# Copying a block's attention sums from PSUM with ScalarE or with VectorE, in 21 steps of a two-attention kernel

## Chip, cores and metric

The kernel runs on one core of one Trainium2 chip. Its time is that of one execution on the device in microseconds (us), and the figure for a kernel is the median of several executions. The profile is of one more execution.

## Reference

Two attentions over separate inputs, each S = 2048 positions by D = 576, with 32 heads of 18 columns. Their outputs stand side by side, so the result is 2048 x 1152. All of it is float32.

```python
# A: each position sees itself and 7 earlier ones, two apart
off = jnp.arange(8) * 2
idx = pos[:, None] - off[None, :]
logits = einsum("bhsd,bhswd->bhsw", q, k[idx]) * Dh ** -0.5   # masked where idx < 0
a = einsum("bhsw,bhswd->bhsd", softmax(logits), v[idx]) @ wo
# B: full attention
scores = einsum("bhqd,bhkd->bhqk", q, k) * Dh ** -0.5
b = einsum("bhqk,bhkd->bhqd", softmax(scores), v) @ wo
return concatenate([a, b], axis=-1)
```

Both begin with qkv = x @ wqkv (576 x 1728). A is called the local attention below.

## The kernel before, in words

**First phase** (to about 450 us): all projections, with each operand split into two parts whose products are added up, so that float32 accuracy is kept on TensorE. Queries, keys and values go to DRAM and come back in the layout of the second phase. The first maxima of the second phase are already made beside the projections.

**Second phase**: 512 steps. The 32 heads are 8 groups `g` of four; the queries are 4 blocks `b` of 512; the keys are 16 tiles `kt` of 128. Step 16 (4 g + b) + kt handles one tile of keys for one block of queries and four heads:

- `score` (L370 to L403) makes four products of keys and queries, 128 x 512 each, into PSUM banks. ScalarE takes the exponentials of them: two scores go through one bank each ("single", L398), two through a double bank and one instruction ("pair", L401).
- `maximum` and `first_part` (L322 to L362, reductions at L256, L258 and L272) make scores of a later block once more, and VectorE reduces them to maxima over the keys, which that block's exponentials need. An ordinary step has three of these: two whole ones ("A" and "B", one on each half of TensorE's rows, r = 0 and 1) and one in two halves ("D" then "E", where E holds the reduction, L272).
- `weigh` (L867 to L874) multiplies the exponentials of the step before with the values: four products (L870) into four partition ranges of the PSUM tile `po`, summed over the 16 key tiles. There is one `po` only. A row of ones in the values makes the softmax denominator.

The order in an ordinary step is written out by hand in `PLAIN = "D1AzwE2B"` (L48; digits and letters w to z are scores), followed by the weigh of the step before. TensorE's rows are used in two halves, so that two matmuls run at once. The banks go round in fixed rings in such steps.

When the sixteenth weigh of a block is through, which is in step 16 (4 g + b + 1), `finish` (L876 to L912) is called in the same step. It copies `po` to the tile `o` (two buffers) in SBUF, and the next weigh, which starts `po` anew, has to wait for that copy. Then, by an agenda: SyncE loads the denominators out of `o` one step later (L904), VectorE inverts them 8 steps later, GpSimd multiplies `o` by them 18 steps later (L908), and the parts are stored to DRAM. The very last block goes another way (`closing`), so 31 blocks are copied.

**Output products of A.** GpSimd does most of the local attention; its results come back from DRAM as tiles `at` (L1090) and are multiplied with the output weights by `sums_of_a` (L1100 to L1119): two halves of the sum (L1211) in two banks, one for each half of the rows. ScalarE copies one half (L1110), VectorE adds the other (L1114). Such a product stands in a step of its own choice of order, from `ROWS` (L50), and `TURNS` (L56) lists the steps in which it may stand, among them every step 16 n: the step in which a block is also copied. `producing` collects the steps that have such a product, from the local attention (L1150) or, in the last group, from B's own output product. The exponentials of the local attention (L1041) take two steps of ScalarE's time, one if a product stands there.

In the steps with a product, `in_turn` (L1217) merges the two halves' queues of instructions: it keeps a clock for each half of TensorE's rows and for ScalarE and VectorE, in which `filled` and `emptied` (L157 to L168) book estimated durations, and always takes the half that could go first. `bank` (L95) then takes the bank that comes free first by these clocks. So a number booked for an engine can change the order and the banks in later steps of this kind.

Of the kernel before, what the change touches and what calls it, by code (L numbers as in the profile page):

```python
# [10 lines left out]
AF = mybir.ActivationFunctionType  # L11
# [40 lines left out]
GAP = 55  # L52

A_FROM = 10
# [4 lines left out]
def ap(t, *dims):  # L59

    return bass.AP(tensor=t.tensor, offset=t.offset, ap=[list(t.ap[0])] + [list(d) for d in dims])


def rows(t, *dims):

    return bass.AP(tensor=t.tensor, offset=t.offset, ap=[list(d) for d in dims])
# [3 lines left out]
def two_attentions(ctx: ExitStack, tc, xa, wa, woa, xb, wb, wob, out):  # L70
# [5 lines left out]
    nc = tc.nc  # L76
# [77 lines left out]
    def held_as(t):  # L154
        return next((n for n, h in held.items() if h is t), None)
# [6 lines left out]
    def emptied(engine, ns, r, t):  # L162

        busy[engine] = max(busy[engine], busy[r] + 214) + ns
        n = held_as(t)
        if n is not None:
            del held[n]
            freed[n] = busy[engine] + 100  # L168

    po = p_po.tile([128, 512], F32, name="po")  # L170
# [10 lines left out]
    step = 0  # L181

    def later(n, f):
        agenda[step + n].append(f)

    def plan(start, pieces):
        for n, f in pieces:
            agenda[start + n].append(f)
# [319 lines left out]
    with (tc.tile_pool(name="x", bufs=1, side="right") as xp,  # L508
# [346 lines left out]
        step = 0  # L855
# [11 lines left out]
    def weigh(*steps):  # L867
        for g, b, kt, es in steps:
            for i in range(4):
                nc.tensor.matmul(po[32 * i : 32 * i + 19], vs[g][:, kt, 19 * i : 19 * i + 19], es[i],  # L870
                                 start=kt == 0, stop=kt == NT - 1)
        busy[0] = busy[1] = max(busy[0], busy[1]) + 870 * len(steps) + 332
        if kt == NT - 1:
            finish(g, b)  # L874

    def finish(g, b):  # L876
        o = work.tile([128, 512], F32, name="o", bufs=2)
        if g == NG - 1 and b == NB - 1:
            return closing(b, o, work.tile([128, 512], F32, name="rec", bufs=1))
        nc.vector.tensor_copy(o, po)  # L880
        emptied("DVE", 598, 0, None)
        den = work.tile([128, 16], F32, name="den", bufs=2)
        rec = work.tile([128, 512], F32, name="rec", bufs=1)
        parts = []

        def room():
            if g == NG - 1 and b == 0:

                parts[:] = [ap(work.tile([128, 4, 128], F32R, name=f"at{i}", bufs=1), (1, 512)) for i in range(2)]
            else:  # L890
                n = work.tile([128, 2, 512], F32R, name="n", bufs=1)
                parts[:] = n[:, 0], n[:, 1], n
            return parts

        if g == NG - 1 and b > 0:
            return shortly(b, o, rec, *room()[:2])

        def store():
            if g < NG - 1:
                load(do[:, g, :, 512 * b : 512 * b + 512].rearrange("i p n -> p i n"), parts[2].bitcast(F32))  # L900
            else:
                plan(step, full(b, parts))

        for at, f in ((1, lambda: load(den, o[DH:128:32])),  # L904
                      (8, lambda: nc.vector.reciprocal(den, den)),
                      (9, lambda: load(drec[g, b].rearrange("i (p n) -> (i p) n", n=16), den)),
                      (13, lambda: load(rec, rows(drec[g, b], (512, 4), (0, 32), (1, 512)))),
                      (18, lambda: nc.gpsimd.tensor_mul(o, o, rec)),  # L908
                      (19, lambda: nc.gpsimd.tensor_copy(room()[0], o)),
                      (20, lambda: nc.gpsimd.tensor_sub(parts[1], o, parts[0])),  # L910
                      (26, store)):
            later(at, f)  # L912

    def shortly(b, o, rec, hi, lo):

        def halved(cols):
            nc.gpsimd.tensor_copy(hi[:, cols], o[:, cols])
            nc.gpsimd.tensor_sub(lo[:, cols], o[:, cols], hi[:, cols])


        cols = [slice(256 * i, 256 * i + 256) for i in range(2)]
        apart = b == 1
        for i in range(2):
            later(1 + i * apart, lambda i=i: nc.vector.transpose(rec[:, cols[i]], o[:, cols[i]]))
        later(1 + 2 * apart, lambda: divided(rec))
        for i in range(2):
            later(1 + (3 + i) * apart, lambda i=i: nc.vector.transpose(o[:, cols[i]], rec[:, cols[i]]))
            later(1 + (3 + i) * apart, lambda i=i: halved(cols[i]))
        plan(step, [(at + 2, f) for at, f in full(b, (hi, lo))])
# [15 lines left out]
    def closing(b, o, rec):  # L945

        n = work.tile([128, 2, 512], F32R, name="n", bufs=1)
        first(3, b, 1)
        for t in range(4):
            if t % 2 == 0:  # L950
                inverse(po, rec, slice(128 * t, 128 * t + 256), o)
            cols = slice(128 * t, 128 * t + 128)
            hi, lo = n[:, 0, cols], n[:, 1, cols]
            nc.scalar.activation(hi, o[:, cols], AF.Copy)
            nc.gpsimd.tensor_sub(lo, o[:, cols], hi)
        for t in range(4):
            end(t, b, (n[:, 0], n[:, 1]))
# [4 lines left out]
    producing = set()  # L962
# [325 lines left out]
    def full(b, new):  # L1288
        def half(t, h):
            if total - int(sum(given)) > 4:  # L1290
                inside.append(lambda: among(*quarter(t, h)))
            else:
                waiting.append(lambda: alone(*quarter(t, h)))

        def among(queues, end):
            behind_scores.append(end)
            return queues

        def quarter(t, h):
            if h == 0:  # L1300
                ys[t, b] = work.tile([128, D], F32, name="y", bufs=4)
            if h == 1:
                later(1, lambda: load(out[512 * b + 128 * t : 512 * b + 128 * t + 128, D:], ys[t, b]))
            return sum_of(ys[t, b][:, 288 * h : 288 * h + 288], t, h, [*olds[b], new])

        return [(4 + 2 * t + h, lambda t=t, h=h: half(t, h)) for t in range(4) for h in range(2)]
# [137 lines left out]
```

## Time and profile before

| | |
|---|---|
| median of 3 runs | 1590.14 us (1588.71 to 1592.66) |
| profiled execution, its own time | 1589.66 us |
| its span in the trace | 1587.8 us |
| TensorE busy | 1577.4 us |
| VectorE busy | 1399.7 us |
| ScalarE busy | 1180.6 us |
| GpSimd busy | 961.6 us |
| copies of `po` (L880), VectorE | 31, 21.3 us busy, 689 ns each |

PE in the rows is TensorE's matmul, PEld its weight load, DVE VectorE, ACT ScalarE, POOL GpSimd, SP SyncE; SPq is SyncE's instruction queue. A row of the timeline gives start and length in us, engine, line, operation, out<-in with the shapes, and how many instructions of the kind were merged into the row; in brackets the engine's idle time ahead of it and what ended that. Matmuls are pipelined, two at once on the two row halves, so the length of a merged PE row isn't the sum of its parts. In the chain of waits a row is what the last chain of work went through.

### The profile page before, as it was taken

What the parts mean: (1) busy time and instruction counts of PE and PEld (TensorE: products, weight loads), DVE (VectorE), ACT (ScalarE), POOL (GpSimd) and SP (SyncE); (2) the same over time, 40 slices, a digit from 0 to 9 for tenths busy, and PEclk for the clock granted to TensorE, in tenths of its full rate; (3) what the DMA queues carried; (4) which work ended last, traced back from release to release, by engine and by line L of the source; (5) the groups of instructions that cost most, each with busy time, mean ns of one, the idle gap of its engine ahead of it and who ended that gap; (6) DMA issues with size and microseconds to landing.
All of it is one profiled execution on the core that took longest, in us unless ns stands there. A gap on an engine that the chain in (4) does not pass through costs nothing.

```text
span 1587.8 us, 34762 instructions
## 1 busy us (share of the span) xinstructions
PE 1577.4 (99%) x13436; PEld 971.1 (61%) x13436; DVE 1399.7 (88%) x2381; ACT 1180.6 (74%) x1912; POOL 961.6 (61%) x816
## 2 busy tenths in 40 slices
PE   9999999999999999999999999999999999999998
PEld 7999999999544444444444445444445445455776
DVE  5299999999999999999998999999999999999433
ACT  6324441121699999999998999999999999998444
POOL 2305752201157997994994995995995997940100
PEclk9999999999999999999999999999999999999999
DMA  9848954532322253253236225324613232234211
GB/s 258 222 142 207 274 171 124 146 98 76 75 52 58 63 115 90 69 127 113 60 83 167 52 76 134 104 50 107 143 53 91 70 87 78 61 125 157 85 39 60
DMA packets 190149, 173.12 MB, mean 109 GB/s; under 512 B 123120, under 2 KB 136944, under 8 KB 188256
## 3 DMA queue, kind: packets, MB, share of 16 engines
q1 hardware_dynamic: 185120, 159.36, 36.1%
q0 software_dynamic: 4032, 10.63, 3.2%
q8 instruction: 105, 1.72, 0.5%
q10 hardware_dynamic: 832, 0.92, 0.2%
q14 instruction: 60, 0.49, 0.1%
HBM read 97.47 MB, written 72.95 MB: 107 GB/s over the span
## 4 chain that ended last, share of the span: by engine, by line
PE 97%; DVE 2%; DMA 1%; issue 0%; ACT 0%; POOL 0%; SPq 0%; ACTq 0%; DVEq 0%; POOLq 0%
PE po L870 31%; PE bank L239 20%; PE bank L491 17%; PE bank L388 10%; PE bank L1211 8%; PE pair L388 7%; PE bank L424 4%; DVE mx L256 1%; DMA at<-dao 0%; DVE mx L272 0%; DVE o L880 0%; PE bank L643 0%; DVE mx L258 0%; DMA out<-y 0%; PE bank L1189 0%
## 5 line engine op out<-in xcount | busy, mean ns | idle before, releaser
L239 PE MATMUL bank<-ks,qs 54*128 54x256 f32 (+1 forms) x2526 | 754.6, 372 | 1.0 <-ACT ohi L819 0.9
L256 DVE TENSOR_REDUCE mx<-bank 128x1 f32<-128x512 f32 x1024 | 680.1, 684 | 63.8 <-PE bank L239 39.6
L239 PEld LDWEIGHTS bank<-ks,qs 54*128 54x128 f32 x2526 | 414.2, 184 | 424.3 <-DVE mx L272 305.0
L398 ACT ACTIVATE e<-bank 128x512 f32<-128x512 f32 x1024 | 610.1, 602 | 71.5 <-PE bank L388 64.4
L870 PE MATMUL po<-ee,v 128*19 128x512 f32 x2048 | 537.1, 599 | 1.0 <-DVE o L880 0.2
L870 PE MATMUL po<-e,v 128*19 128x512 f32 x2048 | 531.8, 599 | 0.0
L401 ACT ACTIVATE ee<-pair 128x1024 f32<-128x1024 f32 x478 | 487.2, 1019 | 0.9 <-PE pair L388 0.3
L388 PE MATMUL bank<-qs,ks 56*128 56x512 f32 x1092 | 461.0, 442 | 0.0
L258 DVE TENSOR_REDUCE mx<-bank 128x2 f32<-128x512 f32 x546 | 356.5, 684 | 19.5 <-PE bank L239 6.6
L272 DVE TENSOR_REDUCE mx<-bank 128x2 f32<-128x512 f32 x478 | 326.1, 682 | 0.0
L388 PE MATMUL pair<-qs,ks 56*128 56x512 f32 x956 | 248.7, 396 | 0.0
L388 PEld LDWEIGHTS bank<-qs,ks 56*128 56x128 f32 x1092 | 194.6, 184 | 15.9 <-ACT e L398 9.0
L1062 POOL TENSOR_TENSOR pr<-lg,akv 128x1024 f32<-128x1024 f32 x72 | 157.0, 2200 | 0.6
L819 ACT ACTIVATE ohi<-bank 128x512 f32<-128x512 f32 (+1 forms) x56 | 30.4, 595 | 156.4 <-issue 129.1
L388 PEld LDWEIGHTS pair<-qs,ks 56*128 56x128 f32 x956 | 138.1, 185 | 0.1
L870 PEld LDWEIGHTS po<-ee,v 128*19 128x19 f32 x2048 | 69.6, 96 | 112.0 <-issue 108.1
L491 PE MATMUL bank<-xhi,ahi 64*128 64x512 f32 (+1 forms) x448 | 120.2, 390 | 0.0
L491 PE MATMUL bank<-xhi,alo 64*128 64x512 f32 (+1 forms) x448 | 114.5, 390 | 0.0
L491 PE MATMUL bank<-xlo,ahi 64*128 64x512 f32 (+1 forms) x448 | 108.8, 391 | 0.1
L1014 POOL TENSOR_TENSOR pr<-aq,akv 128x1024 f32<-128x1024 f32 x40 | 87.8, 2202 | 18.3 <-PE bank L239 17.1
L1064 POOL TENSOR_TENSOR pr<-pr 128x512 f32<-128x512 f32 x72 | 91.1, 1285 | 0.6
L539 POOL TENSOR_TENSOR alo<-raw,ahi 128x512 fp32r<-128x512 f32 (+1 forms) x14 | 17.6, 1257 | 117.4 <-ACT ahi L538 86.0
(206 smaller groups left out, 2383.7 us busy)
## 6 DMA issues: line engine op xcount, KB each, us to landing
do<-n SPq DMA_DIRECT2D x28, 512.0 KB
da<-ohi SPq DMA_DIRECT2D x52, 256.0 KB
akv<-da SPq DMA_DIRECT2D x64, 175.5 KB
out<-y SPq DMA_DIRECT2D x32, 288.0 KB
qs<-dqk SPq DMA_DIRECT2D x30, 288.0 KB
ks<-dqk SPq DMA_DIRECT2D x30, 288.0 KB
at<-dao SPq DMA_DIRECT2D x64, 128.0 KB
rec<-drec SPq DMA_DIRECT2D x29, 256.0 KB
```

The source lines that it names most:

```text
L239: return nc.tensor.matmul(ps, qs[rows_, b, p, 128 * t : 128 * t + 128], ks[rows_, p, 512 * k + at : 512 * k + at + n], start=True, stop=True)
L256: nc.vector.tensor_reduce(mx[:, r, p, t, k : k + 1], ps, axis=AX.X, op=ALU.max)
L258: nc.vector.tensor_reduce(mx[:, r, p, t, 2 * k - 2 : 2 * k], ps.rearrange("q (h n) -> q h n", h=2), axis=AX.X, op=ALU.max)
L272: nc.vector.tensor_reduce(mx[:, :, p, t, 2 * k - 2 + i], ps.rearrange("q (h n) -> q h n", h=2), axis=AX.X, op=ALU.max)
L388: nc.tensor.matmul(ps, ks[at, p, 128 * kt : 128 * kt + 128], qs[at, b, p], start=True, stop=True)
L398: nc.scalar.activation(e, ps, AF.Exp, scale=SCALE)
L401: nc.scalar.activation(whole, both_scores[0], AF.Exp, scale=SCALE)
L491: nc.tensor.matmul(ps, a, b, start=start, stop=stop)
L870: nc.tensor.matmul(po[32 * i : 32 * i + 19], vs[g][:, kt, 19 * i : 19 * i + 19], es[i], start=kt == 0, stop=kt == NT - 1)
L1062: nc.gpsimd.tensor_mul(at, ap(st["lg"], (0, 2), (SUB, W), (1, SUB)), window(st["v"], n))
L1064: nc.gpsimd.tensor_add(at[:, :, :4], at[:, :, :4], at[:, :, 4:])
L1211: nc.tensor.matmul(sums_[r], a, b, start=i == 0, stop=i == len(both[r]) - 1)
```

## The change

In `finish`, the copy of `po` goes to ScalarE in those steps that are in `producing`, but for the steps in which the local attention's exponentials stand: `step - A_FROM - 35` is a multiple of `GAP` (55) there. With it goes the booking in the planner's clocks: 490 ns for ScalarE instead of 598 ns for VectorE.

```diff
@@ finish
         o = work.tile([128, 512], F32, name="o", bufs=2)
         if g == NG - 1 and b == NB - 1:
             return closing(b, o, work.tile([128, 512], F32, name="rec", bufs=1))
-        nc.vector.tensor_copy(o, po)
-        emptied("DVE", 598, 0, None)
+        if step in producing and (step - A_FROM - 35) % GAP:
+            nc.scalar.activation(o, po, AF.Copy)
+            emptied("ACT", 490, 0, None)
+        else:
+            nc.vector.tensor_copy(o, po)
+            emptied("DVE", 598, 0, None)
```

Of the 31 copies 21 move: those of steps 112, 128, 144, 176, 192, 208, 224, 240, 256, 288, 304, 336, 352, 368, 384, 400, 416, 432, 448 and 464, and that of step 496 in the last group. The copy of step 320 stays on VectorE, since the local attention's exponentials stand there, and so do nine more in steps without a product. Lines from 884 on have a number higher by 4 in the changed kernel.

On ScalarE the rows around step 128, before:

```order
L398 ACTIVATE e_10126<-bank_10124 128x512
L398 ACTIVATE e_10130<-bank_10128 128x512
L1110 ACTIVATE y<-bank_10143 128x288
L398 ACTIVATE ee_10179<-bank_10177 128x512
L398 ACTIVATE ee_10179<-bank_10181 128x512
L398 ACTIVATE e_10203<-bank_10201 128x512
L401 ACTIVATE ee_10210<-pair 128x1024
L398 ACTIVATE e_10218<-bank_10216 128x512
```

The same place on ScalarE in the changed kernel:

```order
L398 ACTIVATE e_10126<-bank_10124 128x512
L398 ACTIVATE e_10130<-bank_10128 128x512
L1114 ACTIVATE y<-bank_10143 128x288
L398 ACTIVATE ee_10179<-bank_10177 128x512
L398 ACTIVATE ee_10179<-bank_10181 128x512
L881 ACTIVATE o<-po 128x512
L398 ACTIVATE e_10203<-bank_10201 128x512
L401 ACTIVATE ee_10210<-pair 128x1024
L398 ACTIVATE e_10218<-bank_10216 128x512
```

The copy stands behind the product step's four exponentials (the last two are the `ee` rows) and ahead of the next step's first.

On VectorE the rows at step 128, before:

```order
L256 TENSOR_REDUCE mx<-bank_10155 128x1
L256 TENSOR_REDUCE mx<-bank_10165 128x1
L1114 TENSOR_TENSOR y<-bank_10141,y 128x288
L880 COPY o<-po 128x512
L256 TENSOR_REDUCE mx<-bank_10205 128x1
L272 TENSOR_REDUCE mx<-bank_10199 128x2
L256 TENSOR_REDUCE mx<-bank_10220 128x1
```

The same place on VectorE in the changed kernel:

```order
L256 TENSOR_REDUCE mx<-bank_10155 128x1
L256 TENSOR_REDUCE mx<-bank_10165 128x1
L1118 TENSOR_TENSOR y<-bank_10141,y 128x288
L256 TENSOR_REDUCE mx<-bank_10205 128x1
L272 TENSOR_REDUCE mx<-bank_10199 128x2
L256 TENSOR_REDUCE mx<-bank_10220 128x1
```

The copy is gone there, and the reductions A, E and B of the next step follow the product's addition at once.

TensorE's rows stand in the same order as before except in step 210, the second half of the output product that begins in step 208. The first of its rows before (`wohi`, `wolo` are the two parts of the output weights, `at` those of the local attention's result):

```order
L1211 MATMUL bank_13030<-wohi,at_12640 128x288
L1211 MATMUL bank_13030<-wohi,at_12644 128x288
L1211 MATMUL bank_13030<-wolo,at_12640 128x288
L1211 MATMUL bank_13034<-wohi,at_12640 128x288
L1211 MATMUL bank_13030<-wohi,at_12640 128x288
L1211 MATMUL bank_13034<-wohi,at_12644 128x288
```

And in the changed kernel:

```order
L1215 MATMUL bank_13030<-wohi,at_12640 128x288
L1215 MATMUL bank_13030<-wohi,at_12644 128x288
L1215 MATMUL bank_13033<-wohi,at_12640 128x288
L1215 MATMUL bank_13030<-wolo,at_12640 128x288
L1215 MATMUL bank_13033<-wohi,at_12644 128x288
L1215 MATMUL bank_13030<-wohi,at_12640 128x288
```

The second row half's product, the one in bank_13034 and now bank_13033, begins one matmul earlier. GpSimd's and SyncE's rows stand as before.

## Prediction

> **What bounds the kernel now.** I read the page first, its busy shares and its chain.
>
> ```profile
> PE 1577.4 (99%) x13436; PEld 971.1 (61%) x13436; DVE 1399.7 (88%) x2381; ACT 1180.6 (74%) x1912; POOL 961.6 (61%) x816
> PE 97%; DVE 2%; DMA 1%; issue 0%; ACT 0%; POOL 0%; SPq 0%; ACTq 0%; DVEq 0%; POOLq 0%
> ```
>
> TensorE is on the chain for 97% of the span. A copy on VectorE or ScalarE therefore costs only what it makes TensorE wait, and a 99% busy TensorE can hide such waits, because matmuls of two row groups overlap. So I measure in steps: from the start of one step's four products into po (L870, "the weigh") to the start of the next. The timeline shows an ordinary step:
>
> ```profile
> 692.98 0.60 PE L870 MATMUL po<-ee,v 128*19 128x512 f32 x1
> 692.99 1.02 ACT L401 ACTIVATE ee<-pair 128x1024 f32<-128x1024 f32 x1
> 693.23 0.68 DVE L272 TENSOR_REDUCE mx<-bank 128x2 f32<-128x512 f32 x1
> 693.82 1.48 DVE L256 TENSOR_REDUCE mx<-bank 128x1 f32<-128x512 f32 x2
> 693.89 1.20 ACT L398 ACTIVATE e<-bank 128x512 f32<-128x512 f32 x2
> 694.99 0.61 PE L870 MATMUL po<-ee,v 128*19 128x512 f32 x1
> ```
>
> A step lasts 694.99 - 692.98 = 2.01 us. In it VectorE makes three reductions, which I call E (L272), B and A (the two merged L256), and ScalarE three exponentials: the pair (L401), the second single score's, and the next step's first single (the merged L398). Both are full as well. TensorE writes each score or maximum into a bank that one of these must have emptied; the last two matmuls ahead of a weigh wait for B of the step before (VectorE) and for the second single exponential (ScalarE). Here B starts 1.17 us ahead of the weigh (693.82 to 694.99) and that exponential 1.10 us ahead (693.89).
>
> Now the step in which a block ends beside an output product, with the weigh that ends the block at 680.80:
>
> ```profile
> 680.80 0.61 PE L870 MATMUL po<-e,v 128*19 128x512 f32 x2
> 680.88 1.08 ACT L398 ACTIVATE ee<-bank 128x512 f32<-128x512 f32 x2
> 681.26 0.59 PE L870 MATMUL po<-ee,v 128*19 128x512 f32 x1
> 681.48 0.45 DVE L1114 TENSOR_TENSOR y<-bank,y 128x288 f32<-128x288 f32 x1
> 681.99 0.69 DVE L880 COPY o<-po 128x512 f32<-128x512 f32 x1
> 682.38 0.60 ACT L398 ACTIVATE e<-bank 128x512 f32<-128x512 f32 x1 [0.41 <-PE bank L388]
> 682.60 0.68 DVE L256 TENSOR_REDUCE mx<-bank 128x1 f32<-128x512 f32 x1
> 682.80 0.61 PE L870 MATMUL po<-e,v 128*19 128x512 f32 x2
> 682.87 1.02 ACT L401 ACTIVATE ee<-pair 128x1024 f32<-128x1024 f32 x1
> 683.19 0.68 DVE L272 TENSOR_REDUCE mx<-bank 128x2 f32<-128x512 f32 x1
> 683.78 1.14 ACT L398 ACTIVATE e<-bank 128x512 f32<-128x512 f32 x2
> 683.79 1.37 DVE L256 TENSOR_REDUCE mx<-bank 128x1 f32<-128x512 f32 x2
> 684.96 0.61 PE L870 MATMUL po<-ee,v 128*19 128x512 f32 x1
> ```
>
> The step after the copy is on time (680.80 to 682.80, 2.00 us): po is free at 682.68, before TensorE wants it. The price comes one step later: 682.80 to 684.96 is 2.16 us. The copy pushes A to 682.60, A pushes E to 683.19 (0.39 us after its weigh, against 693.23 - 692.98 = 0.25 in the ordinary step), E pushes B to 683.79, and the weigh follows 1.17 us after B. I took that second step behind all 19 ordinary places of this kind as windows, weigh to weigh. A row has the window and its length, then the busy time and instructions of TensorE, its weight loads, VectorE, ScalarE and GpSimd:
>
> ```profile
> 682.80:684.96 2.16, 2.16 (x19) 1.03 (x17) 2.16 (x4) 2.16 (x5) 2.10 (x3) 1.00 0.45 70
> 717.11:719.43 2.32, 2.32 (x19) 1.00 (x17) 2.32 (x6) 2.32 (x5) 0.73 (x1) 1.00 0.64 145
> ...
> sum 41.30, PE 41.30 PEld 19.38 DVE 41.23 ACT 41.24 POOL 35.77; mean PE 2.17 PEld 1.02 DVE 2.17 ACT 2.17 POOL 1.88
> ```
>
> They take 41.30 us, against 19 x 2.01 = 38.19: the copies cost 3.11 us in all, 0.16 each. VectorE is busy for 41.23 of it and ScalarE for 41.24. That is what decides this change: work goes from a full engine to a full engine.
>
> **The change part by part.** Of 31 copies 21 move: the 19 above, the one in step 208, and the one of the last group's block (step 496).
>
> Removed, on VectorE: 19 x 0.69 us. Without the copy VectorE is free at 681.48 + 0.45 = 681.93. A's bank is filled on time; A ran 0.60 us ahead of E in the ordinary step, so it starts at about 682.80 + 0.25 - 0.60 = 682.45, and A, E and B fall back to their places. Small reductions that stood behind the copy (two more in the window of 2.32 us: six instructions instead of four) fit ahead of A. What VectorE adds to these steps goes from 3.11 us to nothing.
>
> Added, on ScalarE, one copy of the same size. The row for that operation, and two of them back to back:
>
> ```profile
> L819 ACT ACTIVATE ohi<-bank 128x512 f32<-128x512 f32 (+1 forms) x56 | 30.4, 595 | 156.4 <-issue 129.1
> 305.41 1.09 ACT L819 ACTIVATE ohi<-bank 128x512 f32<-128x512 f32 x2 [6.47 <-issue]
> ```
>
> One lasts 0.60 us, and the next may start 1.09 - 0.60 = 0.49 us after it. [...]
>
> When can it start? The last matmul into po ends at 681.26 + 0.59 = 681.85 and VectorE, free by then, started at 681.99, 0.14 us after. I take the same for ScalarE. Nothing else holds it, since its second exponential of the product step starts 0.49 us after 680.88 and leaves the engine at about 681.86. So the copy starts at 681.99, 1.19 us after the weigh. Queued behind it is the next step's first single exponential, which now starts at 682.38 after 0.41 us of idle time: the copy fills that gap and 0.10 us more, so the exponential goes to 682.48. The pair's follows 0.49 later (as 682.38 to 682.87), at 682.97, and the second single's 0.91 later (682.87 to 683.78), at 683.88. This is 1.08 us after the weigh of 682.80, against 693.89 - 692.98 = 0.91 in an ordinary step.
>
> What does a late second exponential cost? Behind the local attention's exponentials (L1041, ScalarE too) there is a step that shows it:
>
> ```profile
> 510.45 0.60 PE L870 MATMUL po<-ee,v 128*19 128x512 f32 x1
> 511.51 1.14 ACT L398 ACTIVATE e<-bank 128x512 f32<-128x512 f32 x2
> 512.21 0.18 PEld L388 LDWEIGHTS bank<-qs,ks 56*128 56x128 f32 x1 [0.15 <-ACT e L398]
> 512.65 0.60 PE L870 MATMUL po<-ee,v 128*19 128x512 f32 x1
> ```
>
> There it starts 511.51 - 510.45 = 1.06 us after the weigh, TensorE's load waits for it by name, and the step lasts 2.20 us, 1.14 after the exponential's start. A second case has 1.10. It is step 320, where such an exponential stands beside the product, and whose copy stays on VectorE:
>
> ```profile
> 1102.47 0.61 PE L870 MATMUL po<-e,v 128*19 128x512 f32 x2
> 1103.43 1.17 ACT L398 ACTIVATE e<-bank 128x512 f32<-128x512 f32 x2
> 1104.53 0.60 PE L870 MATMUL po<-ee,v 128*19 128x512 f32 x1
> ```
>
> So the second step becomes 1.08 + 1.10 = 2.18 us, or 2.22 with 1.14. The nearer row is the first, since the exponentials here last 0.60 us as in step 320. I take 2.18: 19 x 2.18 = 41.42, against 41.30. **The sum over the 19 places is +0.1 us**: the wait for VectorE's reduction becomes one for ScalarE's exponential, of the same length. Bounds: if ScalarE waits for nothing behind po, the copy starts as soon as the engine is free, at 681.86, 0.13 earlier; the first exponential then stays at 682.38 and the second starts 0.98 after its weigh, 2.08 each, -1.8 us. With 1.14 and nothing else it is 2.22, +0.9 us.
>
> The copy also frees po: it ends at 681.99 + 0.60 = 682.59, before VectorE's 682.68, so the next weigh at 682.80 keeps its cover of about 0.2 us. SyncE's load of the denominators waits for o and gets it as early as now; GpSimd's multiplication comes 18 steps later.
>
> Step 208 stands apart. In the chain a transfer is in front of it, and the timeline has these rows behind:
>
> ```profile
> 846.14 6.49 DMA at<-dao
> ```
>
> ```profile
> 857.76 0.69 DVE L880 COPY o<-po 128x512 f32<-128x512 f32 x1 [1.10 <-PE po L870]
> 858.65 0.61 PE L870 MATMUL po<-e,v 128*19 128x512 f32 x2
> 863.07 0.60 PE L870 MATMUL po<-ee,v 128*19 128x512 f32 x1
> ```
>
> TensorE waits for the product's operand until 846.14 + 6.49 = 852.63, whatever the copies do. Step 210, whose row order and banks the planner changes since it now charges ScalarE, runs from 858.65 to 863.07, 4.42 us. I give it between -0.3 (VectorE's queue 0.6 us shorter at its start) and +0.3 (the other order), and take -0.1. In step 496 both engines wait for TensorE for microseconds around the copy, so it costs nothing:
>
> ```profile
> 1513.33 0.69 DVE L880 COPY o<-po 128x512 f32<-128x512 f32 x1 [1.07 <-PE po L870]
> 1515.27 0.60 ACT L398 ACTIVATE e<-bank 128x512 f32<-128x512 f32 x1 [4.48 <-PE bank L388]
> ```
>
> Sum: +0.1 - 0.1 = 0.0 us on the profiled execution's 1589.66 (span 1587.8). The median of the runs shown is 1590.14, 0.5 above, so the forecast is **1590.1 us**.
>
> **The rivals.** First, ScalarE has room. Its share is 74% against 88%, and its idle 0.41 us nearly covers the copy. If the exponentials catch up, the second step falls to step 320's 1104.53 - 1102.47 = 2.06 us: 19 x (2.17 - 2.06) = 2.1 us less, 1588.0. Against it stands the spacing of the rows: 0.49 + 0.91 + 0.49 = 1.89 of 2.01 us are taken in each step, so only 0.12 us can be made up. [...]
>
> Second, slower: the copy holds ScalarE's queue longer. It is the first of that engine's instructions to need po, and the order shows that it also waits for DMA queues and GpSimd, which it must see as done for the buffer o; VectorE had mostly seen them. If these are taken one by one after po is ready, at the 0.14 us that one wait took above, the second step goes to 2.32 and the total up by 19 x 0.15 = 2.9 us: 1593.0. It decides from a copy that starts later than 1.19 us after its weigh. For it: nothing in the old trace shows such a wait on ScalarE. Against it: they were over long before, and the sequencer can pass them while the exponentials of the product step run.
>
> Third, the change hardly acts, because the time is set elsewhere: the transfer ahead of step 208 swallows what the five places before it gain or lose, at most 5 x 0.16 = 0.8 us. This lies inside the forecast's own range, in which I count it.
>
> **How the numbers follow.** The swap of one wait for the other: 0.55, with 1588.0 to 1591.3 as its own range (the bounds -1.8 - 0.3 and +0.9 + 0.3). ScalarE has room, 1588.0: 0.25. Longer hold, 1593.0: 0.15. Anything else, a stall of some transfer above all: 0.05. The range goes from 1587.0 (all 3.1 us won) to 1593.0, and 1 us further at both ends, since the median of three runs that lie between 1588.71 and 1592.66 can itself be off by so much. A measurement of this kernel can tell 0.3% from no change, 4.8 us: faster would need more than the whole 3.1 us that the copies cost, so 0.03; slower needs the second rival with 0.25 us at each place, 0.06; the rest, 0.91, is the same.
>
> **What would show it.** VectorE: L272 0.25 us after the weigh again in the second steps. ScalarE: the copy 1.19 us after its weigh, the next exponential 0.10 later than now, the second single's 1.08 after the following weigh. TensorE's wait in these steps put down to the exponential instead of the reduction; the 19 windows near 41.4 us. The first rival shows as windows under 40, the second as a copy at 1.3 us or later. I am wrong altogether if the steps two or more behind the copy change, since I hold that the backlog is gone after one.

## The result and the profile after

The changed kernel takes **1586.43 us**, the median of 22 runs (1585.16 to 1591.13), against 1589.95 of 22 runs of the kernel before (1587.18 to 1595.28): ratio 0.998, 95% interval 0.9973 to 0.9987. That is 3.5 us off, or 0.2%: small, but the interval leaves out no change. It lies in the predicted range, but not where I put the likeliest case. The profiled execution's span is 1584.6 us, 3.2 under that of before. First the page's shares and chain:

```profile
PE 1574.5 (99%) x13436; PEld 952.6 (60%) x13436; DVE 1387.6 (88%) x2360; ACT 1189.3 (75%) x1933; POOL 961.2 (61%) x816
PE 96%; DVE 2%; DMA 1%; issue 0%; ACT 0%; POOL 0%; SPq 0%; ACTq 0%; DVEq 0%; POOLq 0%
```

VectorE has lost 12 us and ScalarE gained 9, and the chain reads as before. The shares tell nothing of where 3 us went, so I set the two timelines side by side, weigh by weigh. The place at step 128 in the changed kernel, as the timeline shows it:

```profile
680.41 0.61 PE L870 MATMUL po<-ee,v 128*19 128x512 f32 x1
680.46 1.08 ACT L398 ACTIVATE ee<-bank 128x512 f32<-128x512 f32 x2
681.58 0.60 ACT L881 ACTIVATE o<-po 128x512 f32<-128x512 f32 x1
682.04 0.69 DVE L256 TENSOR_REDUCE mx<-bank 128x1 f32<-128x512 f32 x1 [0.55 <-PE bank L239]
682.07 0.59 ACT L398 ACTIVATE e<-bank 128x512 f32<-128x512 f32 x1
682.40 0.61 PE L870 MATMUL po<-e,v 128*19 128x512 f32 x2
682.55 1.03 ACT L401 ACTIVATE ee<-pair 128x1024 f32<-128x1024 f32 x1
682.65 0.68 DVE L272 TENSOR_REDUCE mx<-bank 128x2 f32<-128x512 f32 x1
683.38 0.18 PEld L239 LDWEIGHTS bank<-ks,qs 54*128 54x128 f32 x1 [0.85 <-DVE mx L272]
683.45 1.11 ACT L398 ACTIVATE e<-bank 128x512 f32<-128x512 f32 x2
684.56 0.61 PE L870 MATMUL po<-ee,v 128*19 128x512 f32 x1
```

This is the swap that was predicted, within 0.03 us: the copy 1.17 us after its weigh (681.58 - 680.41; predicted 1.19), E back at 0.25 us after the next (682.65 - 682.40), the second single exponential at 1.05 (683.45 - 682.40; predicted 1.08), and the step 2.16 us long as before. VectorE now waits 0.55 us for TensorE ahead of A. One sign did not come: the idle time that the profile names on TensorE's side is that of the weight loads, and it is still put down to a reduction (L272 in the row of 683.38), not to the exponential. That ScalarE sets the pace here is read from its busy time in the windows. The 19 windows behind the ordinary copies, their first three rows and their sum:

```profile
648.01:650.14 2.13, 2.13 (x18) 0.92 (x17) 2.00 (x4) 2.13 (x5) 2.13 (x2) 1.00 0.94 144
682.40:684.56 2.16, 2.16 (x19) 0.94 (x17) 2.04 (x4) 2.16 (x5) 2.10 (x3) 1.00 0.48 86
716.74:718.88 2.14, 2.14 (x19) 0.93 (x17) 2.14 (x5) 2.14 (x5) 0.78 (x1) 1.00 0.51 144
...
sum 40.79, PE 40.79 PEld 17.61 DVE 38.80 ACT 40.79 POOL 35.32; mean PE 2.15 PEld 0.93 DVE 2.04 ACT 2.15 POOL 1.86
```

VectorE is busy for 38.80 us of them, 2.4 less than before, and ScalarE for all of it. The sum fell from 41.30 to 40.79, 0.5 us of the 3.1 that the copies had cost. So most of the gain was made elsewhere, and the timelines name the place: the two steps with the first half of the output product of step 208. Their windows, weigh to weigh, in the kernel before and then in the changed one (the third column from the end is the granted clock):

```profile
849.07:856.25 7.18, 5.73 (x46) 4.00 (x46) 5.26 (x11) 3.01 (x7) 0.00 (x0) 0.82 0.65 185
856.25:858.65 2.40, 2.40 (x18) 0.91 (x17) 1.30 (x3) 1.45 (x3) 0.00 (x0) 0.83 0.32 104
```

```profile
848.91:854.46 5.55, 4.58 (x47) 3.06 (x45) 4.90 (x10) 2.72 (x6) 0.00 (x0) 1.00 0.59 162
854.46:856.47 2.01, 2.01 (x17) 0.89 (x16) 1.34 (x5) 2.01 (x5) 0.95 (x1) 1.00 0.74 262
```

Before, the two took 7.18 + 2.40 = 9.58 us at a mean clock of 0.82, after 5.55 + 2.01 = 7.56 at full clock: **2.0 us**. TensorE's own rows show what happened. `at` comes as two tiles; first before, then after:

```profile
851.87 0.40 PE L1211 MATMUL bank<-wohi,at 64*128 64x288 f32 x2 [0.96 <-ACT e L398]
852.76 0.40 PE L1211 MATMUL bank<-wohi,at 64*128 64x288 f32 x2 [0.49 <-DMA at<-dao]
```

```profile
851.23 0.40 PE L1215 MATMUL bank<-wohi,at 64*128 64x288 f32 x2 [0.48 <-ACT e L398]
852.12 0.40 PE L1215 MATMUL bank<-wohi,at 64*128 64x288 f32 x2 [0.48 <-DMA at<-dao]
```

It waited twice for its operand `at`, 1.45 us in all before and 0.96 after, and only before was the clock at half speed behind that. The first row of each names ScalarE's exponentials, the last of which ends 0.14 us ahead. They are not what is missing. In the other two profiles of the kernel before the same row names the transfer, and with the operand there in time (the run with the load one step earlier, below), the product starts while they still run, to 850.82 + 1.82 = 852.64:

```profile
850.82 1.82 ACT L398 ACTIVATE e<-bank 128x512 f32<-128x512 f32 x3
851.64 0.50 PE L1211 MATMUL bank<-wohi,at 64*128 64x288 f32 x4
```

So 0.5 of the 2.0 us is shorter waiting, and the other 1.5 came behind the wait. The trace's record of the clock before has 0.50 for 3.41 us there, from 853.66 on, behind 1.45 us of waiting in two pieces, 0.96 and 0.49 (more on this in the last section).

### The profile page after: what moved, and what is told of

Its sections match the earlier page's. It is cut to its first block, busy times and chain, and to the rows that moved or that the text cites. A ratio compares the mean times of both kernels' runs of the same rounds, so it can differ in the third digit from the quotient of the medians.

```text
span 1584.6 us, 34788 instructions
## 1 busy us (share of the span) xinstructions
PE 1574.5 (99%) x13436; PEld 952.6 (60%) x13436; DVE 1387.6 (88%) x2360; ACT 1189.3 (75%) x1933; POOL 961.2 (61%) x816
## 4 chain that ended last, share of the span: by engine, by line
PE 96%; DVE 2%; DMA 1%; issue 0%; ACT 0%; POOL 0%; SPq 0%; ACTq 0%; DVEq 0%; POOLq 0%
PE po L870 31%; PE bank L239 20%; PE bank L491 17%; PE bank L388 10%; PE bank L1215 8%; PE pair L388 7%; PE bank L424 4%; DVE mx L256 1%; DMA at<-dao 0%; DVE mx L272 0%; DVE o L884 0%; DMA first<-xb 0%; DVE mx L258 0%; DMA out<-y 0%; PE bank L1193 0%
## 5 line engine op out<-in xcount | busy, mean ns | idle before, releaser
L256 DVE TENSOR_REDUCE mx<-bank 128x1 f32<-128x512 f32 x1024 | 680.6, 684 | 71.3 <-PE bank L239 46.0
L272 DVE TENSOR_REDUCE mx<-bank 128x2 f32<-128x512 f32 x478 | 326.2, 682 | 0.0
L491 PE MATMUL bank<-xhi,ahi 64*128 64x512 f32 (+1 forms) x448 | 116.2, 390 | 0.0
L491 PE MATMUL bank<-xhi,alo 64*128 64x512 f32 (+1 forms) x448 | 110.6, 391 | 0.0
L491 PE MATMUL bank<-xlo,ahi 64*128 64x512 f32 (+1 forms) x448 | 105.0, 392 | 0.1
```

The lines of the kernel that those rows point to most:

```text
L256: nc.vector.tensor_reduce(mx[:, r, p, t, k : k + 1], ps, axis=AX.X, op=ALU.max)
L272: nc.vector.tensor_reduce(mx[:, :, p, t, 2 * k - 2 + i], ps.rearrange("q (h n) -> q h n", h=2), axis=AX.X, op=ALU.max)
L491: nc.tensor.matmul(ps, a, b, start=start, stop=stop)
```

## The experiments

The theories: **stall** (the gain was made by the wait and the clock at step 208, and the copies are worth the 0.5 us of their windows); **copies** (each copy moved saves VectorE's 0.16 us); **place** (the copy and the new order at steps 208 to 210 make it); and **chance** (the stall differs from execution to execution and has nothing to do with the kernel).

### The two kernels again

No edit. The first repeat of the kernel before:

> The kernel before, once more. In its first profile the step that holds the first half of the output product at step 208 took 7.18 us (849.07 to 856.25), with TensorE waiting for the transfer of its operand until 852.63 and the granted clock at 0.50 from about 853.8 to 857.2; in the changed kernel's profile that step took 5.55 us at full clock. Stall theory (the gain is made at this one place): if the place is the same in every execution of a kernel, the step is again 7.0 to 7.3 us with the clock at 0.50. Chance theory (the place differs from execution to execution and has nothing to do with the change): it may as well be 5.5 us. Both expect a ratio of 1.000 within 0.001.

The first repeat of the changed kernel:

> The changed kernel, once more. Stall theory: the step at the product of step 208 is again near 5.5 us at full clock, and the ratio is 0.998 (0.997 to 0.999). Chance theory: the step is 5.5 or 7.2 us as it comes, and the ratio comes from elsewhere. The sum of the 19 windows behind the ordinary copies is 40.8 us by both, within 0.5.

The kernel before a third time:

> The kernel before a third time, for step 208's product: 7.18 and 9.84 us at half clock in its two profiles. If the stall is a property of the kernel, the step is over 7 us at half clock again. If it is chance from execution to execution, it may be 5 to 6 us at full clock. The ratio is 1.000 within 0.001 by both.

The changed kernel a third time:

> The changed kernel a third time, for the same step: 5.55 and 4.75 us at full clock in its two profiles. If the stall is a property of the kernel, the step is under 6 us at full clock again, and if chance, it may be over 7 at half clock. The ratio is 0.998 to 0.9985 by both.

The kernel before gave ratios of 0.9999 (0.9990 to 1.0007) and 1.0007 (0.9994 to 1.0020), the changed one 0.9985 (0.9976 to 0.9994) and 0.9982 (0.9970 to 0.9994). The step of the stall in the two repeats of the kernel before:

```profile
848.98:858.83 9.85, 6.49 (x48) 4.76 (x46) 5.31 (x11) 3.06 (x7) 0.00 (x0) 0.73 0.57 161
```

```profile
849.81:858.42 8.61, 5.97 (x46) 4.45 (x46) 5.23 (x10) 2.77 (x6) 0.00 (x0) 0.80 0.65 182
```

And in the two of the changed kernel:

```profile
853.06:857.81 4.75, 4.32 (x48) 2.98 (x46) 4.75 (x10) 2.72 (x6) 0.00 (x0) 1.00 0.62 187
```

```profile
849.80:855.35 5.55, 4.58 (x47) 3.06 (x45) 4.90 (x10) 2.72 (x6) 0.00 (x0) 1.00 0.60 170
```

In its three profiles the kernel before falls to half clock here, for longer or shorter, and in its three the changed one doesn't. The step's length varies by 2.7 us between executions of the same kernel. (The second profile of the changed kernel took 1589.66 us in spite of its short step: the step begins at 853.06, 3.3 to 4.2 us later than in the other two (849.80 and 848.91), and the mean clock of that execution was 0.998, against 1.000 and 0.999.)

Three profiles of each are few, but the mean clock of every execution of these runs is on record. One stretch of 3.41 us at half clock costs at most 1.7 us of 1588, as an estimate (half of 3.41), so the mean clock of an execution that has one reads 0.999 at most. Of the 115 executions of the kernel before with a recorded clock 41 read 1.000, and of the 44 of the changed kernel 23. So the kernel before does not fall to half clock every time, and the chance theory is right in this. But the 41 take 1588.42 us in the median (1586.92 and up) and the 23 take 1586.23 (1587.18 and down). The two hardly overlap, so there is a difference between the kernels that does not need the half clock. The windows behind the ordinary copies keep their sums, 41.2 and 41.3 against 40.9 and 40.8 us.

### Only the copy of step 208, and all but that one

```diff
-        if step in producing and (step - A_FROM - 35) % GAP:
+        if step == 208:
```

> Only the copy of step 208 goes to ScalarE, 20 others stay on VectorE (the other order of step 210 comes with it). Copies theory (each moved copy saves VectorE's 0.16 us, 19 of them 3.1 us): nearly nothing, 1590 us, ratio 1.000. Place theory (the copy and the order at steps 208 to 210 make the gain): -0.7 us from steps 208 and 209, ratio 0.9995, and -2.3 us, 0.9985, if the stall ahead of it shrinks with it, for which I see no reason, since the copy stands behind it. Stall theory with the earlier copies as its cause: 1.000.

```diff
-        if step in producing and (step - A_FROM - 35) % GAP:
+        if step in producing and (step - A_FROM - 35) % GAP and step != 208:
```

> All copies of the change go to ScalarE but that of step 208, which stays on VectorE with the old order in step 210. Copies theory: nearly the whole gain, 1587.0 us, ratio 0.998. Stall theory with the earlier copies as its cause: the step of the product at 208 is near 5.5 us at full clock and the gain is 1.6 to 2.5 us, 0.9985. Place theory: 0.5 us from the ordinary places, ratio 0.9997, and the stall as before.

Step 208 alone: 1588.06 us, 0.9993 (0.9984 to 1.0001). All but 208: 1587.80 us, 0.9989 (0.9979 to 0.9999). By time they don't separate. Their windows do: 41.26 us with one copy moved, 40.87 with twenty. So in their windows all the copies together are worth 0.4 to 0.5 us, and the copies theory falls. The stall's step was 5.67 and 5.75 us, both at full clock, though the two kernels have no moved copy in common. (The profile of the first is the fastest of its eleven executions, 1586.58 us, so its stall may be shorter than usual.) In the first of them the instructions of every engine stand in the same order up to the stall as before. Neither the earlier copies nor the one behind the stall can therefore be what shortens it, at least not by what an engine does first. As far as one profile of each shows, place falls too; the next runs make it firm.

### The operand earlier

In the kernel before, six steps earlier:

```diff
-            pieces.append((max(at + 1, one - 9) - start, lambda n=n: get(n)))
+            pieces.append((max(at + 1, one - (15 if one == 208 else 9)) - start, lambda n=n: get(n)))
```

> The kernel before, with the operand of the output product of step 208 loaded six steps earlier (in step 193, ahead of the last loads of queries and keys on SyncE's queue). Stall theory: the step with that product falls from 7.2 or 9.8 us to an ordinary 4.1, and the one behind it from 2.4 to 2.0, at full clock: 3.4 us or more off, 1586 us, ratio 0.998 (0.997 to 0.9985), and the changed kernel loses its lead over this one. Copies theory (VectorE's copies cost the 3.1 us): the load gives at most the stall of the changed kernel's profile, 1.4 us, ratio 0.999 to 1.000, and the copies stay worth 3 us.

The same edit in the changed kernel:

> The changed kernel with the same early load. Stall theory: without the stall the change is worth what its windows show, 0.5 us, and 0.3 us more by the order in step 210: the time is 0.5 to 1.2 us under the kernel before with the early load, 1585.5 us, ratio 0.997. Copies theory: 3 us under the kernel before with the early load.

And one step earlier in the kernel before (10 in place of 15), which only passes two loads of keys:

> The kernel before with the same load one step earlier (step 198), which puts it ahead of the last two loads of keys on SyncE's queue and changes nothing else. Stall theory: the transfer lands 1 to 3 us sooner, the idle time stays under that at which the clock fell (1.46 us in all), the step takes 4.1 to 5.5 us at full clock, and the time is 1586.2 to 1587.5, ratio 0.998 to 0.9985, as much as the change gives. Copies theory: nothing but the landing, 0.999 to 1.000.

The results: 1586.22 us, 0.9981 (0.9973 to 0.9990); 1585.89 us, 0.9976 (0.9966 to 0.9985); and 1586.05 us, 0.9976 (0.9968 to 0.9985). The stall's step in the first and the last of them:

```profile
848.86:852.96 4.10, 4.10 (x47) 2.96 (x45) 4.10 (x9) 2.73 (x6) 0.00 (x0) 1.00 0.55 132
```

```profile
849.98:854.08 4.10, 4.10 (x47) 2.96 (x46) 4.10 (x9) 2.75 (x6) 0.00 (x0) 1.00 0.74 188
```

This decides it. With all 31 copies on VectorE and the old order in step 210, one transfer issued earlier gives 3.75 us (1589.97, the kernel before beside it, to 1586.22), as much as the change, and with the stall gone from both kernels the change is worth 0.3 us (1586.22 to 1585.89, which the intervals can't tell from nothing). Their windows still differ by 41.32 - 40.81 = 0.5. With the load early, the scatter goes too: the eleven executions of the last run lie within 1.4 us, the 33 of the kernel before beside it within 9.4. The changed kernel with the early load has the lowest median of all here, but the intervals don't part it from the other two of this group.

How much of the stall is the clock? The kernel before with the early load (both runs) has 11 of 22 executions at a mean clock of 1.000, with a median of 1585.98 us. The 41 executions of the kernel before at 1.000 took 1588.42. So a late operand costs some 2.4 us there without any half clock, and over all executions (1589.73 against 1586.07) 3.7 us. The clock's part is then at most about 1.3 us on average, as an estimate from these medians: the waits may be shorter in the executions at 1.000.

### The operand later, in the changed kernel

```diff
-            pieces.append((max(at + 1, one - 9) - start, lambda n=n: get(n)))
+            pieces.append((max(at + 1, one - (5 if one == 208 else 9)) - start, lambda n=n: get(n)))
```

> The changed kernel with the operand of step 208's product loaded four steps later (step 203), behind the 512 KB store on SyncE's queue. Stall theory: TensorE's idle time ahead of and in the product grows from 1.0 us to 2 us or more, the granted clock falls to 0.50 behind it, and the step takes 8 to 11 us: 3 to 6 us over the changed kernel, ratio to the kernel before 1.000 to 1.003, so the whole lead is gone with all 21 copies still on ScalarE. Copies theory: at most the later landing is lost, and the rest of the lead stays, 0.999.

1589.39 us, 0.9997 (0.9987 to 1.0007): the lead is gone with 21 copies still on ScalarE. The two steps and TensorE's waits, from the windows and the timeline:

```profile
848.60:856.89 8.29, 5.33 (x47) 3.59 (x45) 5.14 (x11) 3.02 (x7) 0.00 (x0) 0.90 0.54 162
856.89:859.72 2.83, 2.83 (x17) 0.90 (x16) 1.14 (x4) 1.78 (x4) 2.01 (x4) 0.69 0.05 20
```

```profile
853.03 0.40 PE L1215 MATMUL bank<-wohi,at 64*128 64x288 f32 x2 [2.60 <-DMA at<-dao]
853.79 0.40 PE L1215 MATMUL bank<-wohi,at 64*128 64x288 f32 x2 [0.36 <-DMA at<-dao]
```

The wait grew by 2 us and the half clock came back in this profile. Three of the run's eleven executions still have a mean clock of 1.000.

### The copy twice on ScalarE, and in halves on both engines

Both stand on the changed kernel with the early load.

```diff
             nc.scalar.activation(o, po, AF.Copy)
+            nc.scalar.activation(o, po, AF.Copy)
```

> The changed kernel with the early load and each of its 21 copies made twice by ScalarE. ScalarE full (the swap): 19 windows or the steps ahead of them longer by 0.49 us each, 9.3 us in all, the windows near 50 us, and the time 8 to 10 us over the same kernel with one copy. ScalarE has room: the first 0.1 to 0.4 us of each are taken by idle time, and the time grows by 2 to 6 us.

1597.28 us, 11.4 over one copy (1.0059 of before, 1.0045 to 1.0072). The step of the copies grew from 2.0 to 2.45 us, and the one behind it to:

```profile
683.57:685.89 2.32, 2.32 (x16) 0.91 (x16) 1.76 (x4) 2.32 (x5) 2.25 (x3) 1.00 0.13 15
...
sum 44.19, PE 44.16 PEld 17.30 DVE 34.07 ACT 44.19 POOL 35.34; mean PE 2.32 PEld 0.91 DVE 1.79 ACT 2.33 POOL 1.86
```

That is 0.45 + 0.18 = 0.63 us for each copy more, the time from the start of the first to that of the second in the timeline (682.29 to 682.92). My 0.49 was too little, since the second copy of the same tile started only behind the first, which lasts 0.60. The two parts don't say the same. Most of the 0.45 us is TensorE's wait for `po`, which the second copy frees later:

```profile
683.57 0.61 PE L870 MATMUL po<-e,v 128*19 128x512 f32 x2 [0.38 <-ACT o L882]
```

It says nothing of ScalarE's room. The 0.18 us does: in the windows behind, ScalarE is busy for all of 44.19 us, as it was for all of 40.81 with one copy, while VectorE is busy for only 34.07.

```diff
-            nc.scalar.activation(o, po, AF.Copy)
+            nc.scalar.activation(o[:, :256], po[:, :256], AF.Copy)
+            nc.vector.tensor_copy(o[:, 256:], po[:, 256:])
```

> The changed kernel with the early load and each of its 21 copies split: ScalarE copies the first 256 columns, VectorE the other 256, at the same time. Both engines full (the swap): ScalarE's 0.28 us fit the 0.41 us that it had idle, VectorE's 0.34 us more delay A by some 0.2 us in place of 0.55, so the 19 windows fall from 40.8 us to 39.0 (38.2 to 39.9), and the time by 1 to 2.5 us against the same kernel with whole copies. ScalarE has room: the whole copy on ScalarE costs nothing already, VectorE's half adds, and the windows stay at 40.8 or grow.

1589.13 us, 0.9999 (0.9989 to 1.0008), 3.2 over the whole copies; the windows took 42.7 us. The timeline shows why this tells nothing of room:

```profile
682.21 0.38 ACT L881 ACTIVATE o<-po 128x256 f32<-128x256 f32 x1
682.63 0.42 DVE L882 COPY o<-po 128x256 f32<-128x256 f32 x1 [0.49 <-ACT o L881]
682.97 0.68 DVE L256 TENSOR_REDUCE mx<-bank 128x1 f32<-128x512 f32 x1
683.11 0.10 PEld L870 LDWEIGHTS po<-e,v 128*19 128x19 f32 x2 [0.32 <-DVE o L882]
```

VectorE's half waits 0.49 us for ScalarE's, so the halves run one behind the other. They last 0.38 and 0.42 us, and VectorE's next instruction starts 0.34 us after its half (682.63 to 682.97), as I had put it; the 0.28 that I had put to ScalarE's was my estimate. A starts 1.93 us after its weigh (681.04 to 682.97), later than with a whole copy on VectorE (680.80 to 682.60), and the next weigh is late on top. The trial missed its question.

## Why the prediction was right and wrong

- **What bounds an ordinary step, and the swap**: right. The copy, the exponentials and the reductions stand within 0.03 us of where they were put, and the step behind each window keeps its sum within 0.2 us over all 19 (42.25 before, 42.41 after), so the backlog is gone after one step. I had +0.1 us and the runs show -0.5. The term that was mis-sized is the price of 2.18 us that I gave to all 19 windows. Fifteen measure 2.13 to 2.16, and the three with six VectorE instructions (2.32, 2.31 and 2.36) fell to 2.14, 2.12 and 2.08. I had written that their small reductions would fit ahead of A, and then priced these three like the rest.
- **The rivals**: "ScalarE has room" comes nearer in time, with 1588.0, but by the wrong mechanism: its sign was windows under 40 us, and they are 40.8; the windows of the double copy confirm it. There was a gain, but all that the moved copies show of it is 0.5 us of 3.5. The longer hold didn't come: the copy starts at 1.17 us, and its two semaphore instructions on ScalarE's queue start at 680.5 and 680.6, while the exponentials of 680.46 to 681.54 run.
- **Step 208**: this is the step that failed. I wrote that TensorE waits for the operand until 852.63, "whatever the copies do", and booked -0.1. The wait is not fixed: it was 0.43 to 3.35 us in the profiles with the load at its old place, and shorter in the changed kernel. And I did not look at what follows it: the granted clock of 0.50 for 3.41 us, which was in the trace of before. The two steps are 7.18 - 4.10 + 2.40 - 2.03 = 3.45 us longer than in the kernel before with the early load (4.10 and 2.03). Of this 1.45 is the wait, and half clock for 3.41 us can make at most 1.7 more, by the estimate above. The rest, 0.3 us, is of a kind that the changed kernel has at full clock: its TensorE is busy for 4.58 us in the first of these steps, against 4.08 with the early load. The third rival had the transfer in it, as a thing that swallows 0.8 us, not as one that makes 3.
- **Step 210**: 4.42 became 4.11 and the step behind it grew from 2.00 to 2.32, so the other order gave nothing.
- **The range**: that 1586.43 us lies in it is luck. Its lower end stood for all 3.1 us of the copies won and 1 us of scatter, and the gain came from a step that I had booked at -0.1. That a measurement can tell 0.3% from no change was my estimate, which no run shows; here 22 runs of each told 0.2%.
- **The sum** of the profiled executions: -2.0 at steps 207 and 208, -0.5 in the windows, about -0.5 by ScalarE's late starts (last section: five of 0.2 gone, one of 0.2 and three that cost some 0.1 each come instead), and -0.3 ahead of the first window. That is 3.3, against 3.2 seen.

What stays open is why the operand lands sooner in the changed kernel. In the eight profiles with the load at its old place, TensorE's two waits sum to 1.45, 3.35 and 2.64 us before the change, to 0.96, 0.43 and 0.97 after it, and to 1.09 and 1.16 in the two partial ones. In these the last load of the operand is issued 2.7 to 3.1 us ahead of the step's first weigh before the change, 3.6 to 4.8 after it, and 3.4 and 3.5 in the partial ones; the transfer takes 6.5, 8.2 and 7.8 us before and 6.6 to 7.0 in the others. So TensorE waits less because the load is asked for sooner, and in part because it lands faster; what moves the issue was not tried. The partial kernels differ from the first in engine order only behind the stall, or in copies 30 us and more ahead of it. Chance in so few profiles can't be excluded for them, and their times lie between.

## What to carry to other kernels

Before the parts of a change are summed, look through the steps for the few that are far too long, and at the granted clock in them: one step of 7 us among steps of 4 outweighed 19 places of 0.16. A wait of TensorE can have a second price behind it, here, by estimate, up to 1.7 us of lost clock for 1.45 us of waiting, and moving one load by one step was worth as much as the whole change. And work that went from one full engine to another gained little here, 0.5 us where the copies had cost 3.1, whatever the two engines' shares of the whole span say.

## What the runs showed of the hardware

**The clock.** It fell in all four profiles in which the waits at the product summed to 1.45 us or more, for 3.41 us (6.83 in the one with 3.35), and in none of the five with 0.43 to 1.16. In the trace's record of the kernel before, each stretch between the clock's first rise and its last fall at the end is a whole multiple of 3.413 us long: 248 at full clock (846.5 us), 1 at half, 214 at full (730.5 us). In that of the changed kernel it is one stretch of 462 (1577.0 us). The run with the late load, in windows of this length from the bounds of its half clock, has one window without a fall behind it and one with it in a row; the first number behind the length is TensorE's busy time, the third column from the end the clock:

```profile
848.39:851.80 3.41, 2.04 (x16) 0.73 (x14) 3.41 (x8) 2.71 (x5) 0.00 (x0) 1.00 0.64 154
851.80:855.22 3.42, 1.83 (x22) 1.65 (x24) 0.76 (x2) 0.00 (x0) 0.00 (x0) 1.00 0.59 198
855.22:858.63 3.41, 3.41 (x21) 1.37 (x18) 1.97 (x5) 1.50 (x3) 1.00 (x1) 0.50 0.17 66
```

TensorE is idle for 1.37 us of the first window, and the next stays at full clock. It is idle for 1.59 of the second, and the third is at half. In the kernel before it is 1.45, and half clock follows:

```profile
850.25:853.66 3.41, 1.96 (x20) 1.54 (x20) 2.65 (x6) 1.35 (x3) 0.00 (x0) 1.00 0.76 215
853.66:857.07 3.41, 3.41 (x24) 2.29 (x25) 1.84 (x3) 1.30 (x3) 0.00 (x0) 0.50 0.53 192
```

So in the late run a wait of 2.60 us (850.43 to 853.03) is split by a bound at 851.80, and no fall follows its first part. Whether this is why 41 executions of the kernel before show no fall was not shown: their traces were not kept. Idle time alone does not tell a fall: in the first phase of the run with all copies but 208's, a window with 1.53 us of it (74.40 to 77.82) was followed by full clock, and the mean clock of that execution was 1.000.

**Late starts on ScalarE, a multiple of 128 instructions apart.** Five steps of the kernel before are 0.2 us too long (120, 237, 440 and 468 with 2.2 us, 383 with 4.3). They are ordinary in the changed one, where step 233 is new. In each the pair's exponential starts 0.2 us late with its engine free. Step 237 before, and then in the changed kernel, where the x2 row holds the two exponentials ahead of the pair's:

```profile
918.51 1.21 ACT L398 ACTIVATE e<-bank 128x512 f32<-128x512 f32 x2
919.82 1.03 ACT L401 ACTIVATE ee<-pair 128x1024 f32<-128x1024 f32 x1
```

```profile
916.47 1.22 ACT L398 ACTIVATE e<-bank 128x512 f32<-128x512 f32 x2
917.59 1.02 ACT L401 ACTIVATE ee<-pair 128x1024 f32<-128x1024 f32 x1
```

From the first row's start to the pair's it is 1.31 us before and 1.12 after. Counted in the trace, with the semaphore instructions, the late one is the 960th, 1472nd, 2112th, 2368th and 2496th of ScalarE's queue before, and the 1472nd (now in step 233) after: all of the form 128 n + 64. At most of the other places of this form nothing shows. With the semaphore instructions ScalarE's queue has 2744 instructions in the trace before and 2792 after, so in the changed kernel these counts fall in other steps. One even hit a moved copy, in step 176 (the 1216th):

```profile
784.43 0.61 ACT L398 ACTIVATE ee<-bank 128x512 f32<-128x512 f32 x1
785.31 0.60 ACT L881 ACTIVATE o<-po 128x512 f32<-128x512 f32 x1 [0.28 <-issue]
```

Its window is the one that grew, from 2.14 to 2.32 us. In the kernel before, an instruction transfer (queue q14 of the DMA view, kind "instruction", one packet of 0.01 MB) starts 0.65 us behind four of the five late starts and 1.26 us behind the fifth. Whether the two belong together no run tests.
